# A fused adaLN block (sliding-window attention, then a gMLP): loads of the head on two queues, half of the gelu sums on ScalarE, and another written-out order

## The chip, the cores and the metric

The kernel runs on one core of a Trainium2 chip. The core has five engines that run their own instruction streams side by side: TensorE (PE, matmuls; its weight loads are listed as PEld), VectorE (DVE), ScalarE (ACT), GpSimd (POOL) and SyncE (SP), which here only issues DMAs. Data lies in SBUF (128 partitions) and matmul results in PSUM, whose eight banks of 512 fp32 columns are all in use. The metric is the time of one execution on the device in microseconds (us), as the median over runs.

## The reference

All tensors are bf16. There are S = 2048 rows of width D = 448. A vector c gives six modulation vectors; then come an attention block and a gMLP block, each with a layernorm in front and a residual behind:

```python
sa, ca, ga, sb, cb, gb = six rows of silu(c) @ w_mod          # [448] @ [448, 6*448]
h = layernorm(x) * (1 + ca) + sa
q, k, v = split(h @ wqkv)                                      # 16 heads of 28
p = softmax(mask(q k^T * 28**-0.5))                            # keys i-255 .. i
x = x + ga * ((p v) @ wo)
h = layernorm(x) * (1 + cb) + sb
z = gelu(h @ w_in)                                             # [2048, 1792], tanh form
z1, z2 = z[:, :896], layernorm(z[:, 896:])                     # over 896 columns
g = w_sp @ z2 + b_sp[:, None]                                  # w_sp is [2048, 2048]
out = x + gb * ((z1 * g) @ w_out)                              # w_out is [896, 448]
```

## The kernel before

**Tiles and stages.** x is held as 16 tiles of 128 rows (`x_sb`), grouped into four blocks `tb` of 512 rows. In the *head*, c is turned into a column by four tiny matmuls (L508), passed through silu (L512, L513), and multiplied by w_mod: the vectors sa and ca as columns (L535, with L540 repeating the last 64 rows of each vector in the upper partitions), the gates as rows (L570). Meanwhile layernorm of block 0 runs: `stats` (L589) takes bn_stats (L592), bn_aggr (L595), variance plus eps (L597), the power −0.5 on GpSimd (L600); `norm` (L606) writes the normalised rows `xn`. TensorE transposes `xn` (L666), and the eviction applies the modulation while it writes `hT` (L678 on ScalarE, L680 on VectorE). `warm` puts filler matmuls (L557) wherever the written order names one; they compute nothing that is used.

**Projections.** The q and k weights are loaded into `wq_st` and copied into `WQK` with every head padded from 28 to 32 columns (`pad`, L583 and L584). For block 0 the first four groups of four heads, q0 to q3, are accumulated side by side, one 128-row chunk of the width after another, so that each chunk of `hT` is used as it comes (L696); all other groups run one after the other (L708). Evictions go to `qT` and `KT` (L718 on ScalarE, L719 on VectorE). V is L756. Blocks 2 and 3 are transposed by DMA on SP instead of TensorE (L468).

**Attention.** For each query tile j and each half of the heads: scores (L832 for the first two tiles, which have fewer than three key tiles, L858 and L867 for the rest), exp on ScalarE (L819), mask by multiplication on VectorE (L874, L894), P·V on TensorE (L901), division into `o_sb` (L915, L917), a DMA transpose into `hT`, the output projection (L926), the residual on VectorE (L931), layernorm of the new row tile, and one more DMA transpose into `hT`, modulated in place per block (L949 ACT, L951 DVE and POOL). Before each normalised tile of blocks 1 to 3 and of the second layernorm, GpSimd computes the shift −mean·rstd for that tile (L614), whichever engine then normalises (L609 on VectorE, which doesn't read it but waits for it, or L616 on GpSimd).

**gMLP.** For two row tiles at a time TensorE computes the z2 half of h @ w_in (L1011, with 64-row weight tiles), ScalarE applies gelu to a tile's 896 columns from a pair of PSUM banks (L1018), VectorE takes the statistics of the 896 columns in two halves (L592), and normalises in place (L1023). z1 is computed transposed (L1032) with gelu at L1040. z2 lies in memory that held w_mod, the staged q and k weights and the attention's `PW`, so no gelu may write before the last P·V is done. The spatial matmuls (L1055) need all sixteen z2 tiles and the transposed w_sp, which SP brings by DMA transposes into `wspA` and `wspB` (L468). Each of 28 results is added to b_sp on VectorE (L1059) and multiplied by z1 on GpSimd (L1062). When a block's seven are done, the output matmuls (L1072) follow, the residual (L1082), and the store (L1087).

**What sets the order.** The code does not issue instructions as it runs through these loops. It records operations with their dependences in a `Sched`, and a string `ORDER` of words `number.engine.slot` says, by hand-stored result, in which order they go to which engine and which PSUM bank or buffer slot they take. An operation that may run on several engines has them as a dictionary. `order` replays the string, `count` and `waits` turn dependences into semaphore waits, `emit` writes each engine's stream. Each stream runs in its order: an instruction that waits holds everything behind it on its engine. The durations in the code are planning figures; with the order stored, they change nothing at run time.

**The head's loads before.** On SP: both halves of block 0 of x (`d_x00`, `d_x01`), the last 64 rows of w_mod's first part (`d_wmAc`), then pieces of the q and k weights; from 7.72 us, when the first part of w_mod has landed, x's block 1, the v weights and the rest of w_mod (`d_wmB`). On ScalarE's queue: `d_wmAa`, c, `d_wmAb`, and two pieces of the q weights. w_in is loaded by SP in three DMAs issued between 69 and 75 us.

Of the kernel before, what the change touches and what calls it, by code (L numbers as in the profile page):

```python
# [19 lines left out]
2.a 24.v 33.g 0.s 25.v 26.v 27.v 36.g 37.g 3.a 1.s 34.g 4.a 31.g 28.v 5.s 35.g 8.a 29.v 38.g 6.s 9.a 7.s 43.a 39.g 53.p.1 54.p.2 55.p.3 44.p.0 130.v  # L20
128.v 131.v 129.v 132.g 45.a 46.a 56.p.4 57.p.5 58.p.6 59.p.7 60.p.2 52.p.1 139.v 137.v 140.v 138.v 133.g 134.v 141.v 136.a.0 142.g 135.a.1 143.v
120.v 145.v.2 108.v 107.v 67.p.3 146.p.2 144.a.3 68.p.0 69.p.4 147.p 150.p.3 40.g 123.g 121.g 122.v 148.v 149.v 151.p 152.a 48.a 70.p.0 71.p.0
154.p.4.5.6.7 155.p 156.p 153.a 158.p 125.g 42.g 160.p 159.p 157.p 162.a 164.a 32.g 41.g 124.g 47.v 10.s 11.s 14.s 127.g 126.v 191.v 192.v 187.v 30.v
49.g 50.g 13.s 15.s 16.s 12.s 161.a 169.p.0 170.a 171.p.1 172.a 346.p.0 347.a.0 163.v 185.v 189.v 186.v 188.v 190.v 51.v 175.p.7 173.p.6 112.p.0
114.p.1 193.g 194.g 199.g 201.g 197.g 200.g.0 195.g 176.v 202.v.1 198.v.2 113.v 196.g.3 350.v 174.a 352.p.0 353.a.1 181.p.7 203.p.0 371.p.0 166.s
167.s 165.s 168.s 17.s 348.v 115.v 206.p.1 177.p.6 204.v 205.v 207.v 109.p.0 372.a.2 373.a 182.a 208.a 378.p.0 379.a.3 380.a 239.v 241.v 243.v 237.v
244.v 110.v 238.v 20.s 19.s 18.s 240.v 242.v 354.v 111.v 178.v 179.p.7 183.p.1 211.p.0 184.v 293.v 356.v 180.v 349.p.0 398.p.0 212.a 351.p 355.p
215.p.1 357.p 400.p.0 209.p.0 399.a.4.0 381.v 291.v 216.v 406.p.0 210.a 245.g 246.g 251.g 252.v.0 358.v 359.v.0 376.v 374.v 253.g 249.g 254.g.1 403.v
221.p.1 213.p.0 383.v 214.v 402.v 294.v 375.p.0 377.p 407.a.5.1 401.a 427.p.0 222.a 408.p.0 382.p 223.p.0 225.p.1 428.a.6.2 435.p.0 409.a 411.v
429.p.0 384.p 258.s 118.g 247.g 250.g.2 256.s 257.s 248.g.3 255.s 262.g 259.g 226.a 436.a.0.3 292.v 224.v 295.v 385.v 386.v.1 229.p.0 227.p.1 404.p.0  # L30
# [71 lines left out]
class Op:  # L102
    def __init__(self, n, ways, deps, prio, take, table, dma, lat, tail):
# [11 lines left out]
        self.end = None  # L115
        self.token = None
        self.turn = False
        self.shape = "full"

        self.hard = set()  # L120
        self.land = None


class Sched:

# [1027 lines left out]
```

## Time and profile before

| | |
|---|---|
| Median of 3 runs | 280.3 us (280.0 to 280.85) |
| Profiled execution, own time | 279.08 us |
| Profiled execution, span from first to last instruction | 277.4 us |
| Granted TensorE clock, mean over the span | 1.000 |
| First projection matmul (L696) | 12.87 us |
| First spatial matmul (L1055) | 156.59 us |
| Last residual (L1082) starts | 274.45 us |

Lines of the profile name the engine, the line of the kernel, the operation, and the output and inputs by the program's names. In a table of groups, "x16 | 14.1, 916 | 7.8 <-PE ps L1011 6.8" reads: 16 instructions, 14.1 us busy in all, 916 ns each on average, 7.8 us of idle time ahead of them, of which 6.8 ended when PE's L1011 did. In the timeline a row begins with its start and its length, and the bracket is the idle time before it with its releaser. In a table of waits the three numbers are the sum, the count and the longest. In the table of windows each engine has its busy time and, in brackets, its instructions; PEclk is the granted clock and the DMA share is the mean busy share of the 16 DMA engines. In the list of DMA issues the last number is the median time from issue to landing. A mean of a group can be longer than the distance between two of its instructions, because an engine's instructions overlap.

### The profile page before, as it was taken

Reading aid. Unit: us, or ns where it says so; the run is one execution under the profiler, and the core shown is the slowest. Engines: PE = TensorE matmul, PEld = TensorE weight load, DVE = VectorE, ACT = ScalarE, POOL = GpSimd, SP = SyncE. Lnnn points to the kernel's source line nnn. Section 1 sums busy time; section 2 is a strip of 40 time slices with the busy share of each in tenths; the row PEclk is TensorE's granted clock in tenths of the full one; section 3 lists DMA queues with packets and bytes.
Section 4 is the critical chain, followed back from the end, with each engine's and each line's share of the span. In section 5 each row is a group of like instructions: output and inputs, shape, how many; then the busy total and the mean of one; then the engine's idle time right before and its main releaser. Section 6 shows DMA issues by size and latency. Waiting matters only on the chain.

```text
span 277.4 us, 7383 instructions
## 1 busy us (share of the span) xinstructions
PE 266.4 (96%) x3198; PEld 140.8 (51%) x3225; DVE 164.4 (59%) x364; ACT 128.2 (46%) x154; POOL 127.2 (46%) x191
## 2 busy tenths in 40 slices
PE   4999999999999999999999999999999999999995
PEld 1636466656576766444444444444444444444452
DVE  5679999989989999679798300300320042025434
ACT  2587999999999999577676600000000000000000
POOL 6831826914725669884949000600571065334110
PEclk9999999999999999999999999999999999999999
DMA  7966142145993666834999999100000000001113
GB/s 208 304 170 205 23 91 47 21 80 96 121 225 79 80 80 97 194 77 83 190 176 205 206 197 187 35 0 0 0 2 0 0 0 2 0 0 56 62 50 99
DMA packets 65843, 26.01 MB, mean 94 GB/s; under 512 B 56466, under 2 KB 64723, under 8 KB 65811
## 3 DMA queue, kind: packets, MB, share of 16 engines
q1 hardware_dynamic: 65168, 24.68, 43.4%
q10 hardware_dynamic: 642, 0.86, 1.1%
q8 instruction: 25, 0.41, 0.6%
q14 instruction: 8, 0.06, 0.1%
HBM read 9.01 MB, written 1.84 MB: 39 GB/s over the span
## 4 chain that ended last, share of the span: by engine, by line
PE 82%; DVE 8%; DMA 4%; POOL 3%; issue 1%; ACT 0%; ACTq 0%; SPq 0%; POOLq 0%
PE ps L1055 35%; PE ps L1032 8%; PE ps L1072 7%; PE ps L1011 6%; PE ps L708 5%; PE ps L901 5%; PE ps L858 3%; DMA hT<-xn 3%; PE ps L926 3%; PE ps L756 3%; PE ps L867 2%; DVE st_all L592 2%; PE ps L557 1%; DMA c_row<-in_c_dram 1%; PE ps L696 1%; POOL hT L951 1%
## 5 line engine op out<-in xcount | busy, mean ns | idle before, releaser
L819 ACT ACTIVATE PW<-ps 128x2048 bf16<-128x2048 f32 (+1 forms) x56 | 67.4, 1242 | 2.9 <-PE ps L867 1.1
L1059 DVE TENSOR_TENSOR tmpg<-ps,bsp_bc 128x512 bf16<-128x512 f32 x28 | 19.1, 691 | 83.4 <-PE ps L1055 69.3
L1062 POOL TENSOR_TENSOR z1T<-tmpg,z1T 128x512 bf16<-128x512 bf16 x28 | 31.9, 1153 | 79.3 <-DVE tmpg L1059 79.3
L1055 PE MATMUL ps<-wspB,z 128*128 128x512 bf16 x218 | 49.5, 379 | 0.3
L1055 PE MATMUL ps<-wspA,z 128*128 128x512 bf16 x220 | 48.8, 379 | 0.3 <-issue 0.2
L874 DVE TENSOR_TENSOR PT<-PW,mask 128x1024 bf16<-128x1024 bf16 x56 | 38.9, 721 | 0.7 <-ACT PW L819 0.7
L1055 PEld LDWEIGHTS ps<-wspA,z 128*128 128x128 bf16 x224 | 21.8, 98 | 26.6 <-issue 0.4
L1055 PEld LDWEIGHTS ps<-wspB,z 128*128 128x128 bf16 x224 | 21.9, 98 | 26.2
L600 POOL TENSOR_TENSOR rs_all<-ve_all,neghalf 128x1 f32<-128x1 f32 (+2 forms) x37 | 23.6, 645 | 3.7 <-DVE ve_all L597 3.0
L1011 PE MATMUL ps<-w_in,hT 64*128 64x448 bf16 x224 | 23.0, 349 | 1.2 <-DVE hT L951 0.6
L901 PE MATMUL ps<-Vaug,PT 128*128 128x32 bf16 x496 | 24.1, 177 | 0.1
L901 PEld LDWEIGHTS ps<-Vaug,PT 128*128 128x128 bf16 x496 | 21.8, 96 | 4.0 <-DVE PT L894 0.6
L1032 PE MATMUL ps<-hT,w_in 64*128 64x512 bf16 x196 | 22.5, 376 | 0.0
L1072 PE MATMUL ps<-w_out_g,z1T 128*128 128x448 bf16 x112 | 22.2, 352 | 0.0
L708 PE MATMUL ps<-hT,WQK 128*128 128x512 bf16 x80 | 20.5, 379 | 1.3 <-issue 0.4
L616 POOL TENSOR_SCALAR xn<-x_sb,rs_all,ve_all 128x448 bf16<-128x448 bf16 x21 | 18.1, 863 | 7.0 <-DMA hT<-xn 6.4
L901 PE MATMUL ps<-Vaug,PW 128*128 128x32 bf16 x224 | 20.1, 176 | 0.0
L592 DVE BATCH_NORM_STATS2 st_all<-x_sb 128x6 f32<-128x448 bf16 x32 | 18.9, 610 | 1.6 <-DMA x_sb<-in_A_x_dram 1.5
L592 DVE BATCH_NORM_STATS2 st_all<-z 128x6 f32<-128x448 bf16 x32 | 18.3, 607 | 1.7 <-ACT z L1018 1.7
L901 PEld LDWEIGHTS ps<-Vaug,PW 128*128 128x128 bf16 x224 | 17.6, 96 | 1.9
L597 POOL TENSOR_SCALAR ve_all<-mv_all 128x1 f32<-128x1 f32 (+2 forms) x20 | 6.6, 334 | 25.1 <-DVE mv_all L595 21.5
L1018 ACT ACTIVATE z<-ps 128x896 bf16<-128x896 f32 x16 | 14.1, 916 | 7.8 <-PE ps L1011 6.8
(101 smaller groups left out, 343.9 us busy)
## 6 DMA issues: line engine op xcount, KB each, us to landing
out_dram<-fin SPq DMA_DIRECT2D x16, 112.0 KB, 1.7
x_sb<-in_A_x_dram SPq DMA_DIRECT2D x3, 448.0 KB, 3.9
wmod<-in_w_mod_dram SPq DMA_DIRECT2D x1, 1344.0 KB, 9.5
w_in<-in_B_w_in_dram SPq DMA_DIRECT2D x1, 1344.0 KB, 8.2
QBD<-qT SPq DMA_DIRECT2D x16, 64.0 KB, 2.5
w_out_g<-in_B_w_out_dram SPq DMA_DIRECT2D x1, 784.0 KB, 4.9
bsp_bc<-in_B_b_sp_dram SPq DMA_DIRECT2D x1, 512.0 KB, 5.0
x_sb<-in_A_x_dram SPq DMA_DIRECT2D x2, 224.0 KB, 4.2
```

What stands on the lines that cost most here:

```text
L592: st = [dve(0.62 if True else 0, lambda e, t=t, ci=ci, s=s: e.bn_stats(st_all[:, slot, t, ci, :], s()), deps(t), prio) for ci, s in enumer ...
L600: rs = pool(0.53 + 0.15 * len(tiles), lambda e: e.tensor_tensor(rs_all[:, slot, a:b], ve_all[:, slot, a:b], neghalf[:, 0:b - a], ALU.pow), ...
L708: m = pe(4 * MMS, [lambda e, h=h, g=g, kc=kc, tb=tb: e.matmul(ps[:, h.slot[0], :], lhsT=WQK[:, kc, 4 * g:4 * g + 4, :].rearrange("p a b -> ...
L819: ex = act(xdur, lambda e, out_ap=out_ap, in_ap=in_ap: e.activation(out_ap(), in_ap(), ACT.Exp, scale=SCALE), [s], v - 8.0 + u, takes, tab ...
L874: return dve(0.70, lambda e: e.tensor_tensor(cols(hp.slot[0] * 2048 + 1024 * k, [[256, 4], [128, 2], [1, 128]]), cols(at_w() + 128 + 192 * ...
L901: fns.append(lambda e, hp=hp, hO=hO, hi=hi, bi=bi, kb=kb, hd=hd, nb=nb, a=at[hi][bi], p_of=p_of: e.matmul(ps[:, hO.slot[0], 32 * hd:32 * h ...
L1011: return lambda e, kc, p0, start, stop: e.matmul(ps[:, hs[t % 2].slot[hf], 0:D], lhsT=hT[p0:p0 + 64, kc, t * 128:(t + 1) * 128], rhs=w_in[ ...
L1032: return lambda e, kc, p0, start, stop: e.matmul(ps[:, hs[b // 2].slot[b % 2], :], lhsT=w_in[p0:p0 + 64, kc, ft * 128:(ft + 1) * 128], rhs ...
L1055: m = pe(16 * MMS, [lambda e, h=h, si=si, ft=ft, tb=tb: e.matmul(ps[:, h.slot[0], :], lhsT=z2[:, si, ft * 128:(ft + 1) * 128], rhs=(wspA i ...
L1059: a = dve(0.7, lambda e, h=h, ht=ht, tb=tb: e.tensor_tensor(tmpg[:, ht.slot[0], :], ps[:, h.slot[0], :], bsp_bc[:, tb * 512:(tb + 1) * 512 ...
L1062: u = pool(1.16, lambda e, ht=ht, ft=ft, tb=tb: e.tensor_tensor(z1T[tb][:, ft, :], tmpg[:, ht.slot[0], :], z1T[tb][:, ft, :], ALU.mult), [ ...
L1072: return [lambda e, ft=ft: e.matmul(ps[:, h.slot[0], 0:D], lhsT=z1T[t // 4][:, ft, (t % 4) * 128:(t % 4 + 1) * 128], rhs=w_out_g[:, ft, :] ...
```

## The change

1. *Head.* The second half of x's block 0 moves to ScalarE's queue, ahead of c and `d_wmAa`; `d_wmAb` moves to SP. All six pieces of the q and k weights are issued by SP and each waits for a half of x to land. The v weights go ahead of the rest of w_mod, which waits for the first modulation matmuls. Two memsets clear the columns behind ca's first 448, and the first modulation matmuls write 128 rows for the last chunk too, so L540's eight are left out there (32 matmuls instead of 40). The written order has 16 fillers ahead of the projections instead of 13: 8 instead of 5 between c's matmuls and the modulation's, then one between the transposes and four behind them.
2. *First groups.* For block 0 the groups accumulated side by side are q0, k0, q1, k1, two groups at a time per chunk, and the rest follow as q2, k2, q3, k3.
3. *Shift.* −mean·rstd is computed inside `stats`, once for a group of tiles (VectorE) or for a single tile (VectorE or GpSimd); `norm` has no operation for it any more.
4. *Gelu sums.* For the eight odd z2 tiles the gelu accumulates its own sum; a small operation makes −mean, ScalarE runs Square over the tile with that as bias and accumulates the sum of squares (its written output goes to a free `fin` slot and isn't used), another small operation makes the variance plus eps, then GpSimd's power and VectorE's normalisation as before. Tiles 0, 4, 8 and 12 keep VectorE's statistics, but GpSimd normalises them. Tiles 2, 6, 10 and 14 are unchanged.
5. *Last tile.* Tile 15's output is computed, added and stored in two halves of 224 columns.
6. *Order.* `ORDER` is another string throughout. In it, two of w_in's three DMAs stand right behind the loads of x instead of at 69 us; one more output-projection tile stands before the first z2 matmul; the hT modulations of the second layernorm are 9 on VectorE, 2 on ScalarE and 5 on GpSimd instead of 4, 5 and 7; and all engines' assignments and PSUM slots may differ.

```diff
-    t_x0 = [load("d_x0%d" % i, "sp", 0.25, ...x_sb[:, 2 * i:2 * i + 2, :]...) for i in range(2)]
+    t_x0 = [load("d_x0%d" % i, ("sp", "act")[i], 0.25, ...x_sb[:, 2 * i:2 * i + 2, :]...) for i in range(2)]
-    t_wmA = [head("d_wmAa", "act", wmod, w_mod, 0, 2, BOTH, -98.99, 5.7)]
-    t_wmA += [head("d_wmAb", "act", wmod, w_mod, 2, 1, BOTH, -98.97, 5.8), head("d_wmAc", "sp", wmod, w_mod, 3, 64, BOTH, -98.96, 5.4)]
+    t_wmA = [head("d_wmAa", "act", wmod, w_mod, 0, 2, BOTH, -98.97, 6.6, least=5.3), head("d_wmAb", "sp", wmod, w_mod, 2, 1, BOTH, -98.97, 4.4),
+             head("d_wmAc", "sp", wmod, w_mod, 3, 64, BOTH, -98.96, 6.2)]
+    for k, (n, cols, at) in enumerate((("q", LO, 7.2), ("k", HI, 8.6))):
+        a, b, c_ = [head("d_w%s%s" % (n, p), "sp", wq_st, A_wqkv, first, rows, cols, -98.95 + 0.03 * k + 0.01 * i, at + 0.3 * i, [t_x0[i % 2]], 4.4)
+                    for i, (p, first, rows) in enumerate((("b", 2, 1), ("a", 0, 2), ("c", 3, 64)))]
+        t_wq.append([b, b, a, c_])
...
+    t_p2b = [dve(0.12, lambda e: e.memset(wmod[:, 0:3, 2 * D:2 * D + 64], 0.0), prio=-97.6),
+             dve(0.1, lambda e: e.memset(wmod[0:64, 3, 2 * D:2 * D + 64], 0.0), prio=-97.5)]
...
-                m = 128 if ch < 3 else 64
+                m = 128 if ch < 3 or not bank_col else 64
...
-    t_mA = pe(1.2, mod_cols(hA, (0, 1), True), [t_wmA, t_sc, t_p2], -60.0, [hA])
+    t_mA = pe(0.92, mod_cols(hA, (0, 1), False), [t_wmA, t_sc, t_p2, t_p2b], -60.0, [hA])
+    for d in t_wmB:
+        d.deps.add(t_mA)
...
-    def stats(slot, tiles, srcs, deps, prio, quick=False):
+    def stats(slot, tiles, srcs, deps, prio, shift=True):
...
-        return [rs, dve(0.1, lambda e: e.scalar_tensor_tensor(...), [rs], prio)]
+        by = lambda e: e.scalar_tensor_tensor(ve_all[:, slot, a:b], mv_all[:, slot, a:b, 0], -1.0, rs_all[:, slot, a:b], ALU.mult, ALU.mult)
+        if b - a > 1:
+            return [rs, dve(0.16, by, [rs], prio)]
+        return [rs, add({"dve": (0.16, by), "pool": (0.33, lambda e: e.tensor_scalar(ve_all[:, slot, a:b], mv_all[:, slot, a:b, 0], rs_all[:, slot, a:b], -1.0, ALU.mult, ALU.mult))}, [rs], prio)]
...
-        nm = pool(0.34, lambda e: e.tensor_scalar(ve, m, z, -1.0, ALU.mult, ALU.mult), deps, prio)
-        op = add({"dve": (0.45, on_dve), "pool": (...)}, [nm], prio, [h])
+        op = add({"dve": (0.42, on_dve), "pool": (...)}, deps, prio, [h])
...
-            hq = [Hold(bA) for _ in range(4)]
+            first = (0, 4, 1, 5)
+            hq = {g: Hold(bA) for g in first}
...
-        for k, g in enumerate(range(4 if tb in FINE else 8)):
+        for k, g in enumerate((0, 4, 1, 5, 2, 6, 3, 7) if tb == 0 else range(4 if tb in FINE else 8)):
...
+    juR = Res(range(2), [(i,) for i in range(2)])
+    BY_POOL = (0, 4, 8, 12)
+    BY_ACT = (1, 3, 5, 7, 9, 11, 13, 15)
...
+            if t not in BY_ACT:
+                g = act(0.92, lambda e, to=to, of=of: e.activation(to(), of(), ACT.Gelu_apprx_tanh), need, v, table="gelu")
+                rs = stats(2, [t], lambda t_: [lambda: z2[:, t_, 0:D], lambda: z2[:, t_, D:2 * D]], lambda t_, g=g: [g], v, t in BY_POOL)
+                if t in BY_POOL:
+                    z2_ready[t] = add({"pool": (1.45, lambda e, t=t: e.tensor_scalar(
+                        z2[:, t, :], z2[:, t, :], rs_all[:, 2, t:t + 1], ve_all[:, 2, t:t + 1], ALU.mult, ALU.add))}, [rs], v)
...
+            g = act(1.1, lambda e, to=to, of=of, total=total: e.activation(to(), of(), ACT.Gelu_apprx_tanh, accum_out=total), need, v, table="gelu")
+            a = small(less, total, -1.0 / FH, 0.0, [g])
+            q = act(1.1, lambda e, t=t, less=less, square=square, hj=hj: e.activation(
+                fin[:, 2 * hj.slot[0]:2 * hj.slot[0] + 2, :].rearrange("p a d -> p (a d)"), z2[:, t, :], ACT.Square, bias=less, accum_out=square), [a], v, [hj])
+            b = small(var, square, 1.0 / FH, EPS, [q])
+            r = pool(0.6, lambda e, t=t: e.tensor_tensor(rs_all[:, 2, t:t + 1], ve_all[:, 2, t:t + 1], neghalf[:, 0:1], ALU.pow), [b, t_nh], v - 0.01)
...
-            h = Hold(bG)
+            for c0, c1 in ((0, D // 2), (D // 2, D)) if t == NT - 1 else ((0, D),):
+                h = Hold(bG)
```

In the changed kernel the operations keep their names; their lines lie a few to some sixty lines further down.

More of the change, by code (lines that the diff above doesn't have):

```diff
@@ L179, in order @@
             if op.land is not None:
-                op.end = max(at + 1.0, op.land)
+                op.end = max(at + op.least, op.land)
                 dma_at = max(dma_at, op.end - 2.0)
@@ L1017, in bass_adaLN_cond__sliding_block__mixer_gmlp__prompt_kernel @@
         for t, h, m in zip((t0, t0 + 1), hs, ms):
[L1018 to L1022 removed]
+            to = lambda t=t: z2[:, t, :].rearrange("p (a d) -> p a d", d=D)
```

208 lines of the change are left out of this document (110 added, 98 removed).

## The prediction

> **What bounds the kernel now.** I read the page's busy shares first, then the chain that ended last, then the table of windows, and last the table of TensorE's waits.
>
> ```profile
> span 277.4 us, 7383 instructions
> PE 266.4 (96%) x3198; PEld 140.8 (51%) x3225; DVE 164.4 (59%) x364; ACT 128.2 (46%) x154; POOL 127.2 (46%) x191
> ...
> PE 82%; DVE 8%; DMA 4%; POOL 3%; issue 1%; ACT 0%; ACTq 0%; SPq 0%; POOLq 0%
> ```
> ```profile
> core 0: us, PE busy (x) PEld busy (x) DVE busy (x) ACT busy (x) POOL busy (x), PEclk, DMA share, GB/s
> 0.00:13.00 13.00, 9.04 (x74) 5.08 (x76) 7.64 (x25) 4.35 (x8) 9.91 (x25) 1.00 0.85 251
> 60.00:99.00 39.00, 38.54 (x993) 25.99 (x996) 37.53 (x81) 37.35 (x41) 19.68 (x32) 1.00 0.71 118
> 99.00:118.00 19.00, 17.95 (x368) 10.63 (x368) 16.04 (x37) 15.41 (x17) 15.18 (x26) 1.00 0.68 128
> 157.00:275.00 118.00, 116.94 (x549) 54.38 (x556) 28.35 (x44) 1.87 (x4) 32.86 (x29) 1.00 0.20 44
> 109.00:157.00 48.00, 46.60 (x459) 21.95 (x460) 38.96 (x107) 32.41 (x49) 32.56 (x63) 1.00 0.82 156
> ```
> ```profile
> PE ps L832 <- ACT KT L718: 0.7, 1, 0.7
> PE ps L1011 <- DVE hT L951: 0.6, 1, 0.6
> PE ps L1011 <- DVE o_sb L917: 0.4, 1, 0.4
> ...
> PE ps L1011 <- ACT PW L819: 0.3, 1, 0.3
> ```
>
> TensorE bounds it. It is 96% busy and 82% of the chain. The windows give four stages. The head (0 to 13) ends when the first projection can start. In attention (60 to 99) TensorE, VectorE and ScalarE are busy 38.5, 37.5 and 37.4 of 39 us: three engines are full at once. In the stretch where attention hands over to the gMLP's first matmuls (99 to 118) TensorE is idle 1.05 us. From 157 on TensorE runs dense, and this change neither adds nor removes work there. So only three things can move the end: an earlier start of the projections, the listed waits (2.0 us together), and a new wait. Work taken from VectorE, ScalarE or GpSimd is worth nothing by itself unless it ends one of those waits.
>
> **The change, part by part.** I count against the profiled execution (span 277.4, own time 279.08). The median of the three runs, 280.3, lies 1.22 above that; I subtract the sum from the median.
>
> *Head.*
>
> ```profile
> 1.32 4.01 DMA c_row<-in_c_dram
> ```
> ```profile
> 4.76 1.16 DVE L592 BATCH_NORM_STATS2 st_all<-x_sb 128x6 f32<-128x448 bf16 x2 [1.54 <-DMA x_sb<-in_A_x_dram]
> 5.68 2.32 PE L557 MATMUL ps<-ident 128*128 128x512 bf16 x5
> 6.04 1.12 DVE L592 BATCH_NORM_STATS2 st_all<-x_sb 128x6 f32<-128x448 bf16 x2
> 7.83 0.60 PE L535 MATMUL ps<-sc_sb,wmod 128*128 128x1 bf16 x13
> 9.27 0.61 PE L557 MATMUL ps<-ident 128*128 128x512 bf16 x1
> 9.73 0.49 DVE L583 COPY WQK<-wq_st 128x448 bf16<-128x448 bf16 x1
> 10.95 1.43 PE L666 MATMUL ps<-ident,xn 128*128 128x128 bf16 x12
> 11.63 1.12 DVE L680 TENSOR_SCALAR hT<-ps,modT 128x512 bf16<-128x512 bf16 x2 [1.40 <-PE ps L666]
> 12.87 3.40 PE L696 MATMUL ps<-hT,WQK 128*128 128x512 bf16 x15
> ```
> ```profile
> x_sb<-in_A_x_dram SPq DMA_DIRECT2D x3, 448.0 KB, 3.9
> ...
> x_sb<-in_A_x_dram SPq DMA_DIRECT2D x2, 224.0 KB, 4.2
> ...
> wq_st<-in_A_wqkv_dram SPq DMA_DIRECT2D x2, 224.0 KB, 6.4
> ```
>
> Taking the second half of x to ScalarE's queue lets it start about 0.5 us sooner (one of two equal transfers that SP issued back to back). VectorE, however, took the second pair of statistics at 6.04, right behind the first pair and its aggregates, so an earlier arrival gains only what VectorE can use: nothing to 0.3 us. TensorE's path is c, three more fillers (8 for 5), the modulation columns (32 matmuls for 40), transposes, first hT. Five fillers took 2.32, less the pipeline tail about 0.43 each, so 8 take 3.4 from about 5.3 to 8.7; the 40 columns run from 7.83 to the filler at 9.27, so 32 take 1.2 and end near 9.8. Behind them stand the same 16 transposes; of the five fillers that stood before, between and behind them, one now stands between and four behind, under the first hT (0.6 on VectorE). So that hT falls at 11.7 to 12.1 against about 12.2. The k weights go the other way. All six pieces of wq and wk now stand on SP behind a wait for x. If x lands at about 5.0 (0.8 and the 4.2 above), issues of 0.6 (the w_in row below) put the larger k piece, the fifth, near 7.5. With a landing between 3.9 (a larger piece of x, at a quieter time) and 6.4 it arrives at 11.4 to 13.9; I take 11.6, nearer the quieter row, because fewer transfers are in flight by then. A copy of 0.49 follows. So the first projection starts at about 12.4 instead of 12.87: −0.4, between −0.9 and +0.9. The two new memsets (under 0.2 us) lie on VectorE while it waits for x.
>
> [...]
>
> *First QK groups.* TensorE waited 0.7 us at 18.0 for a K eviction before the first scores. With the order q0, k0, q1, k1 the first K group is evicted while eight more matmuls (about 1.8 us at 0.227, from the 3.40 of 15) still run, and one eviction takes 0.6. So the wait goes: −0.7. Late next are the first exps on ScalarE, ahead of which no score waits until the PSUM slots are full.
>
> *Shift of the norm, once per group.*
>
> ```profile
> L614 POOL TENSOR_SCALAR ve_all<-mv_all,rs_all 128x1 f32<-128x1 f32 x28 | 13.3, 482 | 1.5
> ```
> ```profile
> 113.53 0.40 DVE L609 TENSOR_SCALAR xn<-x_sb,mv_all,rs_all 128x448 bf16<-128x448 bf16 x1 [1.69 <-POOL ve_all L614]
> ```
>
> 28 GpSimd instructions become 13 on GpSimd and 10 small ones on VectorE (under 0.2 each). This frees about 7 us of GpSimd, whose stall counts in one place. At 111.8 VectorE waits 1.69 us for GpSimd, and what is queued behind it (o_sb, then hT L951) reaches TensorE late: the waits of 0.4 and 0.6, and the 0.3 ahead of the first L1011. One more out-projection tile now stands before the first of these matmuls, so exp and hT have that much longer. The three listed waits are 1.3. VectorE is still full, but its lateness there comes from that one stop; I take −1.2, between −1.6 (the 0.3 more that the window's idle time and the gaps between the groups leave) and +0.5.
>
> *w_in earlier.*
>
> ```profile
> 31.24 6.97 SPq L468 DMA_TRANSPOSE hT<-xn  x4
> ...
> 69.17 0.59 SPq L399 DMA_DIRECT2D w_in<-in_B_w_in_dram  x1
> ```
>
> Two of its three issues (1.2 us) move to about 24 to 26, where SP is idle until 31.24. Its landing (8.2 us) may then press on the transposes there. I count zero, cover being that idle stretch; up to +1 if it is gone.
>
> *Gelu sums.*
>
> ```profile
> L1018 ACT ACTIVATE z<-ps 128x896 bf16<-128x896 f32 x16 | 14.1, 916 | 7.8 <-PE ps L1011 6.8 <-PE ps L901 1.1
> L1040 ACT ACTIVATE z1T<-ps 128x512 bf16<-128x512 f32 x28 | 14.9, 601 | 5.5 <-PE ps L1032 5.5
> L949 ACT ACTIVATE hT<-hT,modT 128x512 bf16<-128x512 bf16 x5 | 3.9, 809 | 2.1 <-DMA hT<-xn 2.1
> ...
> L512 ACT ACTIVATE sc_sb<-ps 128x3 bf16<-128x3 f32 x1 | 0.2, 176 | 0.8 <-PE ps L508 0.8
> ```
> ```profile
> L592 DVE BATCH_NORM_STATS2 st_all<-z 128x6 f32<-128x448 bf16 x32 | 18.3, 607 | 1.7 <-ACT z L1018 1.7
> L616 POOL TENSOR_SCALAR xn<-x_sb,rs_all,ve_all 128x448 bf16<-128x448 bf16 x21 | 18.1, 863 | 7.0 <-DMA hT<-xn 6.4
> ```
>
> VectorE loses 16 of 32 statistics (9.7 us) and gains small ones (16 at about 0.13, in part on GpSimd). ScalarE gains 8 Squares over 896 columns. No row shows one. The gelu of that width takes 0.92; L949, with a bias and a scale from memory, takes 0.21 more than L1040 at the same 512 columns, so one such operand adds 0.1 and a Square comes to 1.02. The accumulated sum is in no row either: between 0 and 0.2 (the smallest activation, L512) on 16 instructions. Together 8.2 to 11.4 us, less three hT modulations that leave ScalarE (2.4): 32.4 becomes 38 to 41 of the 48 us from 109 to 157. It fits in the 12.3 us in which ScalarE waits for TensorE, but a pair of tiles now costs it 1.83 + 1.02 and up to 0.4 for the sums, 2.85 to 3.25, against 2.82 of TensorE's matmuls (the chain's row below), so PSUM pairs come free with little margin: +0.5, between 0 and +1.5. GpSimd's four norms (896 columns, twice 863 ns, about 1.7 each) take 6.9 of what the shifts freed.
>
> *Join and end.*
>
> ```profile
> 118.25 2.82 PE ps L1011 x28
> ```
> ```profile
> 149.65 5.12 DVE L1023 TENSOR_SCALAR z<-z,mv_all,rs_all 128x896 bf16<-128x896 bf16 x10 [0.69 <-POOL rs_all L600]
> 156.59 5.77 PE L1055 MATMUL ps<-wspA,z 128*128 128x512 bf16 x26 [0.16 <-issue]
> ```
>
> The last z is ready at 154.77, 1.8 us before the spatial matmuls start; TensorE, earlier by some 2 us, would meet it. VectorE has 9.7 us less to do in this stage, which covers that. The gap of 0.16 ahead of the row goes: −0.2, up to 0. The tile written in two halves is not the last one executed, and 14 half matmuls replace 7: 0.
>
> Sum: −0.4 −0.7 −1.2 −0.2 +0.5 = −2.0. Attention between 19 and 109 counts 0, within 1.5 either way, because the sums of work on its three full engines stay as they are and only their order changes. 280.3 − 2.0 = **278.3 us**; the profiled execution, 277.1.
>
> **Rivals.**
>
> A: the gains don't reach the end. For it: in 60 to 99 VectorE and ScalarE are as full as TensorE, so a start 1.1 earlier (head and scores) is given back at the first eviction that is late. Against: they start earlier too. Without those 1.1 and with half of the hand-over, −0.6 − 0.2 + 0.5 = −0.3: 280.0.
>
> B, slower: ScalarE becomes the bound in the gelu stage, because it runs in order and a Square waits for its mean, which a small instruction on VectorE or GpSimd makes in between; the gelus behind the Square stand with it, and TensorE runs out of PSUM pairs. The place is 109 to 157. ScalarE has 48 − 30 = 18 us free there (30 is 32.4 less the modulations) and the change puts about 10 in; it decides from 8 us of such waits, 1.0 at each Square, and passes on every us beyond. A mean queued behind one of GpSimd's new 1.7 us norms would give 1.5 at each: 12 + 10 − 18 = 4, and without the friction already in the sum 280.3 − 2.5 + 4.0 = 281.8. For it: VectorE's one wait of 1.69 on a small GpSimd instruction is of just this kind. Against: the new order puts other work between most gelus and their Squares.
>
> C, slower: the k weights land at 13.9. With copy and first matmul the projections start at 14.3, +1.4: 280.3 + 1.4 − 0.7 − 1.2 − 0.2 + 0.5 = 280.1, and with the 1.5 that attention's new order may lose, 281.6. For it: the wq rows took 6.4. Against: they shared the engines with all of x and w_mod.
>
> D, faster: TensorE comes to full speed sooner. The fillers at 5.68 follow one another at 0.43, the projections of 12.87 at 0.227, and the transposes at 10.95 are still slow, though the granted clock reads 1.00 in the window from 0 to 13. An unbroken 3.4 us of fillers ahead of the columns could end the slow stretch near 9 instead of 12, which would halve the 1.4 us of transposes: −0.7 more, 277.6, unless the k weights hold it. [...]
>
> **How the numbers follow.** The forecast of 278.3 (own range 276.9 to 279.5) has 0.47, D 0.08, A 0.16, B 0.17, C 0.12. A measurement tells 0.3%, 0.84 us, from no change: faster is below 279.46, slower above 281.14. Faster takes 0.44 of the forecast, all of D, 0.04 of A and 0.02 of C: 0.58. Slower takes 0.14 of B, 0.07 of C, 0.04 of A and 0.01 of the forecast: 0.26. The other 0.16 are within. The range goes down to all gains with no friction (−0.9 −0.7 −1.6 −0.2 = −3.4, 276.9) and D's half as much again, 276.6; up to B and C with their dear ends, 282.0.
>
> **What would show it.** Right: L696's counterpart starts near 12.4; no wait of the first scores on a K eviction; no wait of 1.69 on GpSimd before a VectorE norm near 111; the spatial matmuls start near 154.7 with ScalarE at 38 to 41 us from 109 to 157; Square near 1.0 us. Wrong: the first projection past 13, waits of the z matmuls on ScalarE over 1 us in total, or spatial matmuls waiting on the last z or wspA.

## The result, and the profile after

The changed kernel takes 277.88 us (median of five runs, 277.34 to 278.3), beside 280.0 (279.42 to 280.85) for the kernel before in the same comparison: ratio 0.9926, 95% interval 0.9899 to 0.9953. In a later comparison on one chip it was 277.99 against 279.52, ratio 0.9947 (0.9924 to 0.9969). So it is faster by 0.5 to 0.7%, 1.5 to 2.1 us. The forecast was 278.3, by a gain of 2.0. The sum came out; most of its terms did not, as this section shows.

The page's head, then the table of windows, of the changed kernel:

```profile
span 275.9 us, 7411 instructions
PE 265.3 (96%) x3202; PEld 140.1 (51%) x3227; DVE 156.4 (57%) x362; ACT 134.7 (49%) x176; POOL 124.5 (45%) x177
...
PE 82%; DVE 10%; POOL 3%; DMA 2%; issue 1%; ACTq 0%; POOLq 0%
```
```profile
60.00:99.00 39.00, 38.56 (x1022) 26.55 (x1015) 37.20 (x81) 37.05 (x40) 24.26 (x38) 1.00 0.41 70
99.00:118.00 19.00, 18.18 (x356) 10.72 (x354) 17.27 (x41) 16.05 (x18) 14.77 (x26) 1.00 0.74 134
109.00:157.00 48.00, 47.84 (x467) 22.84 (x466) 30.53 (x96) 39.55 (x72) 29.61 (x54) 1.00 0.87 137
```

VectorE has 8 us less work, ScalarE 6.5 more, and TensorE bounds the kernel as before. Where the time went is seen by four points of TensorE's timeline. Its table of waits and its rows, of the changed kernel:

```profile
PE ps L721 <- DVE KT L732: 1.4, 1, 1.4
PE ps L914 <- DVE PT L887: 0.7, 1, 0.7
PE ps L707 <- DVE WQK L592: 0.6, 1, 0.6
```
```profile
4.15 0.37 PE L514 MATMUL ps<-one,c_row 1*128 1x1 bf16 x4 [0.30 <-DMA c_row<-in_c_dram]
4.45 2.93 PE L566 MATMUL ps<-ident 128*128 128x512 bf16 x8
7.67 0.95 PE L541 MATMUL ps<-sc_sb,wmod 128*128 128x1 bf16 x32 [0.29 <-DMA wmod<-in_w_mod_dram]
11.26 2.97 PE L707 MATMUL ps<-hT,WQK 128*128 128x512 bf16 x13 [0.60 <-DVE WQK L592]
...
16.32 0.29 PE L845 MATMUL ps<-qT,KT 32*128 32x128 bf16 x8
...
154.92 10.31 PE L1096 MATMUL ps<-wspA,z 128*128 128x512 bf16 x47 [0.16 <-issue]
```

| us | before | after | change |
|---|---|---|---|
| first projection | 12.87 | 11.26 | −1.61 |
| first scores | 18.68 | 16.32 | −2.36 |
| first spatial matmul | 156.59 | 154.92 | −1.67 |
| last residual | 274.45 | 272.80 | −1.65 |

The head gives 1.61 and the first scores another 0.75. From there to the spatial matmuls the changed kernel needs 138.60 us instead of 137.91: it gives 0.69 back, where the forecast had a gain of 0.9 (−1.2 −0.2 +0.5). From the first spatial matmul to the last residual nothing differs (117.9 in both).

The time from first scores to first spatial matmul is called the *middle* below. It is compared between profiles because the head varies: with one and the same head the first projection came between 10.82 and 11.37 in different profiles, and on one chip single executions of the kernel before took 278.0 to 281.1. The changed kernel's middle was 138.40 to 138.60 in five profiles whose first projections lay between 10.70 and 13.95 (its own two, and those of three runs below that alter only the head). The kernel before, again with only the head altered, had 136.98 to 137.91 in three. So the new order's middle is the longer one in every profile. A profile shows one execution, a median many; where the two disagree, this text goes by the median.

### The profile page after: what moved, and what is told of

The parts are those of the page before. It is cut to its first block, busy times and chain, and to the rows that moved or that the text cites. A ratio compares the mean times of both kernels' runs of the same rounds, so it can differ in the third digit from the quotient of the medians.

```text
span 275.9 us, 7411 instructions
## 1 busy us (share of the span) xinstructions
PE 265.3 (96%) x3202; PEld 140.1 (51%) x3227; DVE 156.4 (57%) x362; ACT 134.7 (49%) x176; POOL 124.5 (45%) x177
## 4 chain that ended last, share of the span: by engine, by line
PE 82%; DVE 10%; POOL 3%; DMA 2%; issue 1%; ACTq 0%; POOLq 0%
PE ps L1096 35%; PE ps L1027 8%; PE ps L1073 8%; PE ps L1115 8%; PE ps L721 5%; PE ps L914 4%; PE ps L769 3%; DVE PT L887 3%; PE ps L939 3%; PE ps L871 3%; DMA wmod<-in_w_mod_dram 2%; DVE st_all L601 2%; PE ps L880 1%; PE ps L707 1%; POOL xn L626 1%
## 5 line engine op out<-in xcount | busy, mean ns | idle before, releaser
L1096 PE MATMUL ps<-wspA,z 128*128 128x512 bf16 x219 | 48.1, 379 | 0.4 <-issue 0.2
L887 DVE TENSOR_TENSOR PT<-PW,mask 128x1024 bf16<-128x1024 bf16 x56 | 38.2, 717 | 0.3 <-ACT PW L832 0.3
L609 POOL TENSOR_TENSOR rs_all<-ve_all,neghalf 128x1 f32<-128x1 f32 (+2 forms) x29 | 19.2, 669 | 15.8 <-DVE ve_all L606 14.6
L721 PE MATMUL ps<-hT,WQK 128*128 128x512 bf16 x83 | 21.2, 379 | 2.3 <-DVE KT L732 1.4
L1115 PE MATMUL ps<-w_out_g,z1T 128*128 128x448 bf16 (+1 forms) x119 | 22.5, 341 | 0.0
L1027 PE MATMUL ps<-w_in,hT 64*128 64x448 bf16 x224 | 22.3, 349 | 0.0
L1081 ACT ACTIVATE z1T<-ps 128x512 bf16<-128x512 f32 x28 | 14.8, 616 | 4.9 <-PE ps L1073 4.9
L1115 PEld LDWEIGHTS ps<-w_out_g,z1T 128*128 128x128 bf16 x119 | 11.6, 98 | 10.2
L1027 PEld LDWEIGHTS ps<-w_in,hT 64*128 64x128 bf16 x224 | 10.7, 94 | 10.6 <-issue 0.4
```

What stands on the lines that cost most here:

```text
L609: rs = pool(0.53 + 0.15 * len(tiles), lambda e: e.tensor_tensor(rs_all[:, slot, a:b], ve_all[:, slot, a:b], neghalf[:, 0:b - a], ALU.pow), ...
L721: m = pe(4 * MMS, [lambda e, h=h, g=g, kc=kc, tb=tb: e.matmul(ps[:, h.slot[0], :], lhsT=WQK[:, kc, 4 * g:4 * g + 4, :].rearrange("p a b -> ...
L887: return dve(0.70, lambda e: e.tensor_tensor(cols(hp.slot[0] * 2048 + 1024 * k, [[256, 4], [128, 2], [1, 128]]), cols(at_w() + 128 + 192 * ...
L1027: return lambda e, kc, p0, start, stop: e.matmul(ps[:, hs[t % 2].slot[hf], 0:D], lhsT=hT[p0:p0 + 64, kc, t * 128:(t + 1) * 128], rhs=w_in[ ...
L1096: m = pe(16 * MMS, [lambda e, h=h, si=si, ft=ft, tb=tb: e.matmul(ps[:, h.slot[0], :], lhsT=z2[:, si, ft * 128:(ft + 1) * 128], rhs=(wspA i ...
L1115: return [lambda e, ft=ft: e.matmul(ps[:, h.slot[0], c0:c1], lhsT=z1T[t // 4][:, ft, (t % 4) * 128:(t % 4 + 1) * 128], rhs=w_out_g[:, ft, ...
```

## The experiments

### What made the head shorter

In the profiles of both kernels TensorE's fillers follow one another at 427 ns until it comes to full rate, and at 216 ns from then on. In the kernel before that step lies near 12.2 us, behind the transposes (two fillers at 10.10 took 1.06, two at 12.22 took 0.59); in the changed kernel the sixth of the eight fillers, at 6.56, is already fast, and all that follows (columns, transposes) with it. In a second execution of the changed kernel all eight fillers were still slow and the step came at 8.0, just ahead of the transposes; the first projection came only 0.11 later (11.37):

```profile
4.34 3.60 PE L566 MATMUL ps<-ident 128*128 128x512 bf16 x8
```

So what counts is that the transposes run fast. Two things were different from the kernel before: c's load stood ahead of the 448 KB of w_mod on ScalarE's queue, so that the fillers began at 4.45 instead of 5.68, and they were eight instead of five. Five runs take these apart. Each entry in the table is from the run's profile, the time with the ratio to the kernel before on the same chip.

**c behind w_mod again (changed kernel).** In the written order:

```diff
-... 2.a ... 3.a ...      # c, then d_wmAa
+... 3.a ... 2.a ...
```

> The changed kernel with c's load put back behind the first 448 KB of w_mod on ScalarE's queue. Theory: c lands near 5.4 instead of 4.1, eight fillers at half rate end near 9.0, the modulation matmuls start there instead of at 7.7, and the first projection starts at 12.2 to 12.8 instead of 11.26: 1.0 to 1.5 us later, and the time is 0.7 to 1.5 above 277.9. Rival (the k weights' copy sets the first projection, 0.6 us of wait at 11.26): first projection 11.3 to 11.7 and the time unchanged within 0.4.

**Five fillers instead of eight (changed kernel).**

```diff
-... 60.p.6 61.p.7 69.p.2 70.p.3 71.p.4 72.p.5 54.p.1 ...
+... 60.p.6 61.p.7 69.p.2 54.p.1 ...
```

> The changed kernel with five fillers instead of eight between c's matmuls and the modulation's. Theory (the three more bring TensorE to full rate near 7.0 instead of 10 or 12): fillers at 0.43 us throughout end near 6.7, TensorE stands until w_mod lands near 7.7, transposes run at half rate, and the first projection starts at 11.6 to 12.4 instead of 11.26; the time 0.3 to 1.1 above 277.9. Rival (full rate comes from the earlier start or by chance, not from their number): full rate before 8 again, first projection at 11.26 within 0.2, time unchanged.

**c ahead of w_mod (kernel before).** There c is number 3 and `d_wmAa` number 2.

```diff
-2.a 24.v ... 3.a 1.s ...
+3.a 24.v ... 2.a 1.s ...
```

> The kernel before with one swap on ScalarE's queue: c's load stands ahead of the first 448 KB of w_mod instead of behind it. Theory (the head's gain of 1.6 us came mostly from TensorE reaching full rate early, and c's early arrival is what started its fillers early): c lands near 4.2 instead of 5.3, the five fillers run from about 4.5 to 6.7, the modulation still waits for w_mod until about 7.7, and full rate comes only if five fillers are enough; the first projection starts between 11.9 and 12.9, and the time is 279.0 to 280.0 (before 280.0). Rival (c's place alone makes the head): first projection near 11.6 and the time 278.6 or less. Rival (attention gives any early start back): the first projection earlier by 0.5 or more and the time unchanged within 0.3.

**The same, with six more fillers (kernel before).**

```diff
-... 60.p.2 52.p.1 ...
+... 60.p.2 61.p.3 62.p.4 63.p.5 64.p.6 65.p.7 66.p.2 52.p.1 ...
```

> The kernel before with c's load ahead of the first 448 KB of w_mod, as in the run where TensorE fell back to half rate after standing 2.7 us, and with six more fillers behind the five, so that TensorE doesn't stand. Theory (what the head gains is the early full rate, kept by fillers until w_mod lands): full rate near 5.6, kept, fillers end near 7.6, transposes at full rate, the first projection at 11.5 to 12.5 instead of 12.87 (13.97 with five fillers); the time 0.4 to 1.4 below 279.5. Rival (fillers don't keep it, or they delay the modulation): first projection after 13 and the time 279.5 or more.

**x on one queue (changed kernel).**

```diff
-    t_x0 = [load("d_x0%d" % i, ("sp", "act")[i], ...
+    t_x0 = [load("d_x0%d" % i, ("sp", "sp")[i], ...
```

> The changed kernel with the second half of x's first block back on SP, behind the first half; c then leads ScalarE's queue. Theory (the two queues save only issue time, which VectorE's statistics hide, and what matters in the head is c): c lands 0.2 to 0.6 us earlier, x's second half 0 to 0.5 later, the first projection stays at 11.3 within 0.4 and the time within 0.4 of 278.0. Rival (x on two queues makes the head's gain): first projection later by 0.5 or more and the time by as much.

| | c's matmuls | full rate from | first projection | median, ratio (95%) |
|---|---|---|---|---|
| before | 5.38 | 12.2 | 12.87 | 280.0 |
| changed | 4.15 | 6.6 | 11.26 | 277.88, 0.9926 (0.9899 to 0.9953) |
| changed, c behind w_mod | 6.23 | about 12 | 13.95 | 280.69, 1.0047 (1.0019 to 1.0076) |
| changed, five fillers | 4.25 | 13.1 | 12.21 | 279.49, 0.9992 (0.9971 to 1.0013) |
| before, c first | 3.78 | 5.5, lost again | 13.97 | 279.48, 1.0000 (0.9968 to 1.0032) |
| before, c first, 11 fillers | 3.78 | 6.2 | 10.89 | 277.17, 0.9924 (0.9897 to 0.9952) |
| changed, x on one queue | 3.78 | 6.6 | 10.70 | 277.79, 0.9957 (0.9931 to 0.9982) |

TensorE's timeline with five fillers in the changed kernel, then in the kernel before with c first:

```profile
4.55 2.32 PE L565 MATMUL ps<-ident 128*128 128x512 bf16 x5
7.46 1.01 PE L540 MATMUL ps<-sc_sb,wmod 128*128 128x1 bf16 x32 [0.59 <-DMA wmod<-in_w_mod_dram]
8.39 1.04 PE L675 MATMUL ps<-ident,xn 128*128 128x128 bf16 x8
9.22 0.63 PE L565 MATMUL ps<-ident 128*128 128x512 bf16 x1
9.65 1.06 PE L675 MATMUL ps<-ident,xn 128*128 128x128 bf16 x8
```
```profile
4.08 1.92 PE L556 MATMUL ps<-ident 128*128 128x512 bf16 x5
8.72 0.59 PE L534 MATMUL ps<-sc_sb,wmod 128*128 128x1 bf16 x13 [2.72 <-DMA wmod<-in_w_mod_dram]
...
10.98 1.06 PE L556 MATMUL ps<-ident 128*128 128x512 bf16 x2
11.83 1.49 PE L665 MATMUL ps<-ident,xn 128*128 128x128 bf16 x12
```

With five fillers the modulation starts as early as with eight (it waits for w_mod), but eight transposes take 1.04 instead of 0.61, and the head is 0.95 longer. In the kernel before with c first, five fillers took 1.92, less than the 2.32 of a slow five: full rate had come. Then TensorE stood 2.72 us, and two fillers at 10.98 took 1.06 again: the rate was lost, and the head became longer than before. The granted clock says the same of the two stretches from 5.47 us on (TensorE's busy time, then PEclk; its 1.00 alone proves little, since it reads 1.00 beside the slow fillers of the kernel before too):

```profile
5.47:8.88 3.41, 0.69 (x10) 1.00 1.05 274
8.89:15.70 6.81, 6.81 (x65) 0.50 0.86 296
```

Six more fillers across that gap keep the rate:

```profile
4.08 3.55 PE L556 MATMUL ps<-ident 128*128 128x512 bf16 x11
...
9.57 0.83 PE L665 MATMUL ps<-ident,xn 128*128 128x128 bf16 x12
```

Twelve transposes take 0.83 instead of 1.49, and with the old order otherwise untouched the kernel reaches the gain of the whole change: 0.9924 against 0.9926 and 0.9947. The two profiles exaggerate the fillers' part: that of the run without them shows the slowest of its twelve executions (281.23), the other the fastest of its eight (276.22), and 1.25 us of the 3.08 between their first projections is w_mod itself, since the modulation starts at 8.72 in one and at 7.47 in the other. The medians are 2.3 us apart. Chance alone doesn't explain the early step: of all the profiles here, in each of the nine with c early and eight or eleven fillers the first transposes run at full rate, and in none of the other five.

The direction of each expectation held, but most sizes were too small. The kernel before with c first lay past its range for the first projection (13.97, not 11.9 to 12.9), since the loss of the rate and w_mod's landing, 0.9 later, were not foreseen. With the added fillers it lay past it on the other side (10.89, not 11.5 to 12.5; the time 1.9 below the kernel before on that chip, 2.3 below the run without them, not 0.4 to 1.4). c put back in the changed kernel cost more than foreseen (13.95, not 12.2 to 12.8; the time 2.7 above the changed kernel's on another chip, not 0.7 to 1.5), as c then landed at 6.2 and the full rate came only near 12. Five fillers met their range in the first projection, and the time lay 1.5 above, not 0.3 to 1.1. The x halves bring no gain that shows: with x on one queue c lands earlier, and the head was 0.6 shorter in that one execution (10.70, not 11.3 within 0.4), about as much as it varies by. No run shows that two queues save only issue time, as the expectation for x on one queue had it: from issue to landing x's halves took a median of 4.2 us on one queue (kernel before), and 3.0 and 3.2 on two (changed kernel), with other loads beside them in both.

What sets the moment of the step is not shown. With c early it came between 5.5 and 8.7 us, 1.4 to 4.3 after the first filler behind c (at 13.1 with five fillers in the changed kernel), and it moved between two kernels with the same fillers (6.2 and 7.6) and between two executions of the changed kernel (6.6 and 8.0). The loss came, in the kernel before with c first, with 2.72 us of standing for w_mod: of the 3.41 us ahead of it (5.47 to 8.88, granted clock 1.00), TensorE was busy for 0.69.

### Whether VectorE's wait on the shift made the hand-over wait

**No such wait (kernel before).** GpSimd still computes all 28 shifts.

```diff
+        own = (" %d.v" % (nm.n + 1)) in ORDER.replace("\n", " ")
-        op = add({"dve": ..., "pool": ...}, [nm], prio, [h])
+        op = add({"dve": ..., "pool": ...}, deps if own else [nm], prio, [h])
```

> The kernel before; a normalisation that stands on VectorE no longer waits for GpSimd's shift, which it doesn't read (GpSimd still computes all 28). Theory (the wait of 1.69 us at 111.8 makes TensorE's waits of 0.4 and 0.6 at 114 and 118): these two waits go, the spatial matmuls start 0.7 to 1.2 us earlier than 156.6, the time falls by 0.7 to 1.2, to about 279.0. Rival (VectorE is late there anyway, because three engines are full): TensorE's idle time between 99 and 118 stays near 1.0 us and the time within 0.3 of 280.0.

TensorE's waits in that run, from 0.7 down:

```profile
PE ps L833 <- ACT KT L719: 0.7, 1, 0.7
PE ps L1012 <- ACT PW L820: 0.3, 1, 0.3
PE ps L902 <- DVE PT L875: 0.2, 1, 0.2
```
```profile
19.62 0.29 PE L833 MATMUL ps<-qT,KT 32*128 32x128 bf16 x8 [0.69 <-ACT KT L719]
...
156.19 9.02 PE L1056 MATMUL ps<-wspA,z 128*128 128x512 bf16 x41
```

The waits of 0.6 and 0.4 are gone. The middle is 156.19 − 19.62 = 136.57, that is 1.34 less than before. The spatial matmuls started only 0.4 earlier because in this execution the head was 0.94 longer, with the projections still at half rate. The median, 278.89 against 279.44 (ratio 0.9983, 0.9955 to 1.0012), doesn't tell a gain from none.

The edit is not shown to be what ended the two waits, because they are also absent from the two other profiles of the kernel before in which VectorE still waits for the shift: c first with 11 fillers, and with five. The normalisation that waited 1.69 us in the profile before, in these two:

```profile
111.34 0.40 DVE L608 TENSOR_SCALAR xn<-x_sb,mv_all,rs_all 128x448 bf16<-128x448 bf16 x1 [0.59 <-POOL ve_all L613]
116.03 0.40 DVE L608 TENSOR_SCALAR xn<-x_sb,mv_all,rs_all 128x448 bf16<-128x448 bf16 x1 [0.43 <-POOL ve_all L613]
```

Their middles are 136.98 and 137.60, the second with a wait of 0.9 on a DMA inside attention. So the wait of 1.69 is long in one of three executions of the same code, and what the edit is worth (1.34, 0.41 or 1.03 by these single profiles) is open.

### What the new order gave back

The changed kernel's one long stall lies at 37.2 us: a projection waits for a PSUM bank that VectorE is late to evict. VectorE and GpSimd ahead of it, in the changed kernel's timeline:

```profile
30.96 1.04 POOL L585 TENSOR_TENSOR wo_g<-wo_g,gg_sb 128x448 bf16<-128x448 bf16 x1
31.02 1.00 DVE L613 SCALAR_TENSOR_TENSOR ve_all<-mv_all,rs_all 128x4 f32<-128x4 f32 x1
```
```profile
35.69 1.20 POOL L585 TENSOR_TENSOR wo_g<-wo_g,gg_sb 128x448 bf16<-128x448 bf16 x1
35.91 2.13 DVE L887 TENSOR_TENSOR PT<-PW,mask 128x1024 bf16<-128x1024 bf16 x2
...
37.97 0.68 DVE L732 CAST KT<-ps 128x512 bf16<-128x512 f32 x1
38.93 0.81 PE L721 MATMUL ps<-hT,WQK 128*128 128x512 bf16 x3 [1.38 <-DVE KT L732]
```

L613 works on four columns. It ends at 32.02 with GpSimd's multiplication, which ends at 32.00. Two mask multiplies take 2.13 beside another of GpSimd's, where two elsewhere take 1.28.

**The eviction earlier in VectorE's order (changed kernel).**

```diff
-... 379.v 398.v ... 428.v 224.v ...       # masks, then the K eviction
+... 379.v ... 224.v 398.v 428.v ...
```

> The changed kernel with one eviction of K (block 1, first group) ahead of two mask multiplies in VectorE's order instead of behind them. Theory (VectorE's order holds TensorE's PSUM bank at 37.2 us, 1.5 us of stall, and a stall there is passed on to the end): the eviction ends near 36.7 instead of 38.65, the stall falls to 0.3 or less, and the interval from first scores to first spatial matmul falls from 138.6 by 0.6 to 1.4; the time by as much. Rival (attention is bound by three full engines, a stall removed returns as another): the stall goes, the interval stays within 0.3 of 138.6.

**The multiplications of wo later (changed kernel).**

```diff
-... 120.g 250.g.1 253.g.2 252.g.3 ... 121.g ... 260.g 259.g ...
+... 250.g.1 253.g.2 252.g.3 ... 260.g 259.g 120.g 121.g ...
```

> The changed kernel with GpSimd's last two multiplications of wo by its gate moved from 31 and 36 us to about 44 us, where GpSimd is idle. Theory (VectorE's instruction stands while a GpSimd instruction on whole tiles runs: L613 took 1.00 us instead of 0.16 and ended with GpSimd's, a mask multiply 1.53 instead of 0.68): L613 takes about 0.16, VectorE reaches the K eviction 0.8 to 1.7 us sooner, the stall of 1.5 at 37.2 falls below 0.8, and the interval from first scores to first spatial matmul falls by 0.5 to 1.5. Rival (the long instructions are long for another reason): the durations and the stall stay, the time is unchanged.

**The changed kernel as it is, on the same chip.**

> The changed kernel itself, beside the next three on the same chip. Its head should again show TensorE at full rate before the modulation matmuls, or, if the phase of the step in rate is chance, a later step and a later first projection. From the first scores to the first spatial matmul it should again take 138.6 us (before: 137.9), whatever the head does.

| | middle | first projection | median, ratio (95%) |
|---|---|---|---|
| changed, again | 138.59 | 11.37 | 277.99, 0.9947 (0.9924 to 0.9969) |
| K eviction earlier | 137.80 | 10.82 | 277.08, 0.9913 (0.9886 to 0.9939) |
| wo later | 137.79 | 11.37 | 277.09, 0.9925 (0.9897 to 0.9953) |

With wo later, the same small instruction in VectorE's timeline:

```profile
31.12 0.16 DVE L612 SCALAR_TENSOR_TENSOR ve_all<-mv_all,rs_all 128x4 f32<-128x4 f32 x1
```

0.16 instead of 1.00, with no multiplication of GpSimd's beside it. Each edit removes the stall at 37 and takes 0.8 us off the middle, so a stall there does pass to the end, if not whole: after the first edit a wait of 0.5 on VectorE comes in its place ahead of 38.9, after the second one of 0.7 ahead of 45.7, where the moved multiplications now meet an hT modulation. The kernel before shows such lengthening the other way round: GpSimd's shift at 110.03 took 1.26 us beside two mask multiplies of VectorE from 109.98 to 111.24, and the next one, at 113.23, took 0.26. Why an instruction of one engine is longer beside certain ones of the other is not shown.

**Three moves together (changed kernel).** The two kinds above, wo held until the eviction is done, and a statistics instruction behind two masks at 106.

```diff
-... 252.g.3 ...
+... 252.g.3 120.g 121.g ...               # and 224.v ahead of 398.v, 428.v; 647.v behind 776.v
+    for d in t_wog[2:]:
+        d.deps.add(K_ready[(0, 4)])
```

> The changed kernel with three moves together: the K eviction ahead of two mask multiplies, GpSimd's last two multiplications of wo held until that eviction is done, and one statistics instruction (row tile 10) behind two mask multiplies instead of ahead of them. Theory (each removes a stall of TensorE by VectorE's order or by GpSimd's long instructions, and the three are separate places): no stall near 37, none near 45, the one of 0.75 at 107 falls to 0.2 to 0.4; the interval from first scores to first spatial matmul falls from 138.6 to 136.8 to 137.3 and the time is 276.0 to 276.6. Rival (the two single moves, 0.8 each, removed the same loss): the interval stays at 137.8 and the time near 277.1.

```profile
35.74 3.57 DVE L886 TENSOR_TENSOR PT<-PW,mask 128x1024 bf16<-128x1024 bf16 x3
35.90 2.86 POOL L584 TENSOR_TENSOR wo_g<-wo_g,gg_sb 128x448 bf16<-128x448 bf16 x2 [0.96 <-DVE KT L731]
...
40.01 0.74 PE L768 MATMUL ps<-wv,hT 128*128 128x448 bf16 x3 [1.14 <-DVE Vaug L773]
```

A miss by both expectations: the middle is 138.31, longer than after either single move, and the time 277.58 (0.9945, 0.9923 to 0.9967) is no better than theirs. The multiplications now run beside three masks, which take 3.57 instead of about 1.9, and a V eviction behind them is late by 1.14. The stall at 107 fell from 0.69 to 0.31, as foreseen.

### How much ScalarE can carry in the gelu stage

**Two more Squares of 512 columns behind each of the eight (changed kernel); their results are not used.**

```diff
+    for t in (1, 7, 3, 5, 11, 9, 15, 13):
+        for _ in range(2):
+            prev = act(0.6, lambda e, t=t: e.activation(sc_rep[:].rearrange("p a b -> p (a b)"), z2[:, t, 0:512], ACT.Square), [q_of[t], prev], 0.0)
+            z2_ready[t].deps.add(prev)
```

> The changed kernel with two more Squares of 512 columns behind each of the eight (results unused): some 8 us more on ScalarE between 109 and 157, where it is busy 39.6 of 48. Theory (ScalarE has 8 us of slack there, and its queue, not the work of the change, has been hiding everything so far): it is now full, PSUM pairs come free late, TensorE waits for ScalarE in the z matmuls by 1 to 4 us in total, and the time rises by 1 to 4. Rival (it is bound by TensorE with room to spare): less than 0.5.

ScalarE's new group, TensorE's waits and the granted clock (last but two in each window) in that run:

```profile
L1140 ACT ACTIVATE sc_rep<-z 128x512 bf16<-128x512 bf16 x16 | 10.1, 630 | 0.5
```
```profile
PE ps L1075 <- ACT z1T L1083: 3.8, 2, 2.6
...
PE ps L1075 <- ACT z L1039: 1.9, 2, 1.5
...
PE ps L1028 <- ACT z L1051: 0.9, 1, 0.9
PE ps L1028 <- ACT z L1039: 0.7, 1, 0.7
```
```profile
154.00:158.00 4.00, 3.61 (x22) 1.43 (x24) 2.00 (x5) 2.77 (x6) 3.52 (x7) 0.68 1.20 237
```

288.04 us, ratio 1.0301 (1.0268 to 1.0334): 10.05 us for 10.1 us of work, where 1 to 4 were expected. TensorE waits 7.3 us for ScalarE. Soon after the longest of these waits it runs at a granted clock of 0.50 for 3.41 us (155.45 to 158.86; 0.68 over the window of four), which costs an estimated 1.7 more (half of 3.41). The expectation took ScalarE's 8.4 idle us for slack. But of these, 1.8 lie ahead of the first gelu (a wait for a DMA) and 4.0 behind the last Square, where it waits for the z1 matmuls; only some 2.5 lie among the z2 tiles, where the added work stands. So most of the idle time could carry none of it. One load was tried, with the normalisation of each odd tile waiting for it too: from how little on ScalarE would hold TensorE up is not shown.

### Whether the two gains add

**c first with 11 fillers, and no wait on the shift (kernel before).**

> The kernel before with two edits and its own order otherwise: c's load first with six more fillers, and no wait of VectorE's normalisations on GpSimd's shift. With the fillers alone the interval from first scores to first spatial matmul was 136.98, with the second edit alone 136.57, in the kernel before 137.91. Theory (the two waits that the second edit removes at 114 and 118 were already gone when the head came earlier, so the edits overlap): interval 136.4 to 136.9, first projection near 10.9, time 276.6 to 277.2. Rival (they add): interval 135.6 to 136.0, time near 276.0.

The first projection came at 11.62 (full rate only from 7.6), the first scores at 17.44 and the spatial matmuls at 154.82: a middle of 137.38, outside both expectations. The time is 277.43, ratio 0.9912 (0.9876 to 0.9947), no different from the fillers alone. The gains don't add. With the fillers alone the two waits on VectorE were gone already, so there was nothing at 114 and 118 left to win; why the middle is 0.8 longer than with the second edit alone is open.

## Why the prediction was right, and where it was not

The time (277.88 for 278.3) and its sign were right. That the sum came so close is luck: its terms erred on both sides, the head by −1.2 and the middle by +1.6.

*Head, −0.4: it was −1.61.* The step that failed is "8 take 3.4 from about 5.3 to 8.7": c's landing was taken from the old order of ScalarE's queue, though c had been moved ahead of 448 KB, and the fillers were costed at 0.43 throughout. c came at 4.15, so the fillers were done before w_mod landed, and columns and transposes ran at full rate. Rival D had the mechanism, with a chance of 0.08 and 0.7 us; by the runs it is as large as the change's whole net gain (without the three added fillers 279.49 beside 279.44 for the kernel before; with c first and fillers alone 277.17 beside 279.1). Its 3.4 us, eight fillers at 0.43, are shown by no run to be what the step takes: with c early the step came 1.4 to 4.3 us after the first filler behind c, and only at 13.1 with five fillers in the changed kernel. The k weights were no danger: x's half landed by 3.8, not 5.0, so their copies ended soon enough to cost only 0.6 of wait. C's premise was wrong with it.

*First QK groups, −0.7: −0.75* (5.81 from first projection to first scores, then 5.06), and the wait on the K eviction is gone.

*Shift, −1.2: not shown.* The step took a wait of one execution for a standing cost: two other profiles of the old shift lack TensorE's waits at 114 and 118. They are gone in the changed kernel too, but TensorE's idle time from 99 to 118 falls only from 1.05 to 0.82, since one of 0.69 on a mask at 107 came in their place.

*Attention's order, 0 within 1.5: about +1.6* (138.60 where the terms gave 137.91 − 0.9). Of this, 0.8 is the stall on VectorE at 37, recovered in two ways. The stall at 107 fell by 0.4 in the run with three moves, but no run has that alone. What is left is not traced, and part of it may be that the −1.2 was never there to be had.

*w_in earlier, 0:* no run tried it alone; nothing in the trace waits for it.

*Gelu sums, +0.5: 0.* Square took 1.05 (forecast 1.02), its sum a separate instruction of 0.21 (forecast 0 to 0.2), ScalarE 39.55 (forecast 38 to 41), and TensorE waits for no gelu. B did not come, but was nearer than its price said: it had ScalarE decide from 8 us of further waits and pass on what goes beyond, and 10.1 us of further work cost 10.05. No gain shows either: no wait on VectorE's statistics was among TensorE's waits before.

*Join, −0.2: 0.* The 0.16 is there in both kernels. *Rival A* was wrong in its cause: from first projection to first spatial matmul the changed kernel takes 143.66, 143.68 with c late (first projection at 13.95) and 144.26 with five fillers. Attention passes an early or late head on, nearly whole.

## What to carry to other kernels

Look in the first microseconds at the distance between equal matmuls (here 427 ns, then 216), not at their mean length: a tiny load that lets TensorE begin, and fillers that bridge every wait until the real work, were worth as much here as the whole change with its new order (0.9924 beside 0.9926). Compare stages between fixed points of the timeline, since a forecast's sum can be right while its terms are not. Compare a wait over several executions before counting it as a cost. And count an engine's slack only in the stretch where the added work would stand: idle time ahead of it or behind the last of it carries nothing.

## What the runs showed that was not expected

TensorE lost its full rate after 2.72 us without matmuls in the head of the kernel before with c first, and after 2.58 us in the gelu stage of the run with more Squares (granted clock 0.68 in the window behind). A four-column VectorE instruction took 1.00 us instead of 0.16, and a small GpSimd one 1.26 instead of 0.26, each ending with the other engine's instructions beside it (32.02 and 32.00 in the changed kernel, 111.29 and 111.24 in the kernel before). Accumulating a sum on ScalarE was, in the changed kernel, a second instruction of 0.21 us. 10.1 us of work on an engine that was busy 39.6 of 48 us cost 10.05. And a wait of 1.69 us, the dearest the forecast counted on, was 0.59 and 0.43 in other executions of the same code.
